# An attention and feed-forward kernel: the attention stage rewritten with raw pairwise transposes, K=64 scores and exponentials transposed on TensorE

## The chip, the cores and the metric

The kernel runs on one core of a Trainium2 chip. Its time is the device time of one execution in microseconds (us); lower is better. The kernel before was timed three times: 997.22, 1001.03 and 1001.95 us, with a median of 1001.03 us. Engine names are those of the profile: PE is TensorE's matrix multiply and PEld its weight load, DVE is VectorE, ACT is ScalarE, POOL is GpSimd, and SP is the queue from which the DMAs are issued. L12 is line 12 of the kernel that is spoken of.

## What is computed

There are 8 batches, 8 heads, 576 tokens and 64 columns per head. Each head's output mixes causal softmax attention with a read from a memory matrix, and the joined heads then pass through a feed-forward block.

```python
scores = scale * np.matmul(q, k.transpose(0, 1, 3, 2))      # scale = 1/8, causal mask, row maximum taken off
a = np.exp(scores)
a /= a.sum(-1, keepdims=True) + 1e-09
local = np.matmul(a, v)
q_p = phi(q)                                                # max(q, exp(q) - 1) + 1
mem_out = einsum(q_p, M_prev) / (einsum(q_p, z_prev) + 1e-06)
x = g * mem_out + (1 - g) * local                           # g = sigmoid(beta), per head
# feed-forward over 4608 tokens, 512 -> 1024 -> 512
h = x @ w_in
solu = h * softmax(h)
out = (layernorm(solu) * g_ln) @ w_out
```

The weights w_in and w_out arrive as float64 words, and the kernel decodes them itself.

## The kernel before

Attention is done for one pair of heads at a time: 32 pairs, four to a batch. Of the 576 tokens of a head, 512 form four blocks of 128 rows, and the last 64 rows of both heads form one shared "tail" block. Numbers that need more than one pass of precision are split into a high and a low part: `hi` and `lo` (L318 to L329) write the two parts of k, q and phi(q) side by side, so that a row has 64 high and 64 low columns and the contraction of a matmul is 128 deep.

One pair goes through these steps. `trans` (L437) transposes the split k, q and phi(q) on PE, 27 transposes of 128x128 (L447, L456), and ACT copies them out of PSUM (L433). `swap` makes a second copy of the transposed k with its halves exchanged, by a DMA (L469). `scores` (L523) multiplies q by k (L542) and by the exchanged k (L543); DVE adds the mask, negates, writes the scores to SBUF and finds the row maximum in one instruction (L546). `soft` (L482) takes the exponential and its row sum on ACT (L496), the scale from it on DVE (L500, L502), then the normalised high part in fp16 on POOL (L483) and the low part on DVE (L512), and transposes both by a DMA (L518). `values` (L602) multiplies by v, with v as the stationary operand (L608), and adds phi(q) times M_prev (L616, L635); the result has tokens in its columns, as the feed-forward's first matmul needs it. phi(q) has been divided by its norm beforehand (L348 to L366, on POOL and DVE). `merge` (L593) adds the high and low halves.

The feed-forward works on tiles of 128 tokens, 36 in all. For each, `g1` runs 24 matmuls with a moving operand of 512 columns into `h` (L683); a chain of single instructions follows, c1 to c10: maximum (DVE L698), exponential (ACT L704), product and sum (DVE L709), subtract the mean (POOL L718), squares (ACT L724), a power (POOL L728), the scaled high part (ACT L481) and low part (DVE L736), and a DMA transpose (L742). `g2` runs 24 more matmuls (L755).

Each engine executes its instructions in the order in which they were written. A virtual clock sets that order: `slot(p)` emits the scores of pair p, the values of pair p-1 and the preparation of pair p+1, and puts feed-forward steps in the gaps. Where each part falls is set by a table of fractions of a slot (P, L28 to L52) and of offsets (OFF, L53). PSUM has five banks that everything in attention shares in turn (`ps_s`), one bank for `g2`, and two banks for `h`. The weights are decoded by `weight_step` (L250) during the first slots, 24 chunks through a two-deep staging buffer.

Of the kernel before, what the change touches and what calls it, by code (L numbers as in the profile page):

```python
# [25 lines left out]
# Where the parts are emitted: fractions of a slot (of the slot before a pair's scores for its  # L26
# loads, preparation and transposes), and gaps of chains in us. They order the engines' work.
P = {  # L28
    "ld_k": -0.50, "ld_q": -0.40, "ld_v": -0.25, "ld_b": -0.22,
# [8 lines left out]
}  # L38
DEPS = (
    "ld_k k_hi k_lo tk0 tk1 tt swap", "ld_q q_hi q_lo phi3", "q_lo tt", "q_lo tq0 tq1", "ld_q phi1 phi2 phi3 phi4 phi5 p_hi p_lo tp0 tp1 tp2",  # L40
    "ld_v v1 v2 v3 v4 v5 v6", "v3 phi4", "ld_b m1", "s0 s1 s2 s3 st", "va vb vt", "ld_b phi3",
)
BUFS = {"pe": 5, "ksw": 2, "vst": 3, "mst": 2, "kT": 2, "qT": 2, "pT": 2, "ot": 2, "xf": 2, "lt": 2, "wt": 2}
OFF = {}
WT = ("lt",)
ENG = {"kst": "p", "qst": "p", "pst": "a", "lkst": "p", "lqst": "p", "lpst": "p", "relu": "a", "mx": "v", "v": "d", "h8": "p", "h6": "p", "h4": "p", "h2": "p", "h5": "p", "kT": "a", "qT": "a", "pT": "a", "xh": "a", "out": "a", "ln": "a"}
ENG0 = {}
EARLY = 5
WACT = 1
WPOOL = 1  # L50
P.update({'ld_k': -0.5, 'ld_q': -0.4, 'ld_v': -0.26061662954976644, 'ld_b': -0.1867630925796864, 'k_hi': 0.0, 'k_lo': 0.04, 'q_hi': 0.05, 'q_lo': 0.1, 'phi1': 0.12450449063930862, 'phi2': 0.19, 'phi3': 0.22023831229089622, 'phi4': 0.4, 'phi5': 0.49895318147926565, 'p_hi': 0.56, 'p_lo': 0.5448550353585894, 'v1': 0.01475376331245451, 'v2': 0.047523081121272154, 'v3': 0.12, 'v4': 0.5039851911500934, 'v5': 0.4742918073033215, 'v6': 0.54, 'm1': 0.48, 'tk0': 0.42010190124933844, 'tk1': 0.5017931553145808, 'tt': 0.5105694394820975, 'tq0': 0.56, 'tq1': 0.62, 'tp0': 0.8936934582661713, 'tp1': 0.9, 'tp2': 0.94, 'swap': 0.8808993830957448, 's0': 0.06, 's1': 0.20945219180060937, 's2': 0.4666999403328722, 's3': 0.61, 'sb': 0.04, 'st': 0.8, 'va': 0.07977765073539692, 'vb': 0.2, 'vt': 0.5125215606487175, 'ev': 0.4, 'e': 0.7129860651889, 'ex': 0.8, 'rr': 0.4, 'hi': 0.2752673338051288, 'lo': 1.41333215189741, 'tr': 1.24449487306772, 'mg': 0.2919189879262507, 'mg2': 0.6, 'xl': 0.8, 'c1': 0.2, 'c2': 1.3287303998695392, 'c3': 1.2, 'c4': 1.2, 'c5': 1.6217740235049547, 'c6': 1.1, 'c7': 0.4, 'c8': 0.6, 'c9': 1.1, 'c10': 0.6067076693930333, 'o1': 0.3, 'o2': 1.1498997242258686, 'low': 16.0, 'w0': 4.0, 'wmax': 3.483578790421383, 'wdec': 3.265097220718073, 'spl': 5.0})
# [12 lines left out]
def kernel(
    ctx: ExitStack,
# [843 lines left out]
```

## Time and profile before

| | |
|---|---|
| median of three runs | 1001.03 us |
| span of the profiled execution | 999.8 us |
| DVE busy | 888.1 us |
| PE busy | 809.1 us |
| ACT and POOL busy | 654.0 and 653.6 us |
| mean granted clock of PE | 0.899 |

The profile is of one execution; what lies around its span is not in it, and the span stands 1.2 us below the median. "Busy" is the time in which an engine has at least one instruction in work. The end of a matmul is modelled and includes the time to drain, so that neighbouring matmuls overlap in the rows: what a matmul costs PE is the distance between starts, or a run's length divided by its count. "Idle before" in a row is the engine's waiting ahead of these instructions, with what ended it.

### The profile page before, as it was taken

Reading aid. Unit: us, or ns where it says so; the run is one execution under the profiler, and the core shown is the slowest. Engines: PE = TensorE matmul, PEld = TensorE weight load, DVE = VectorE, ACT = ScalarE, POOL = GpSimd, SP = SyncE. Lnnn points to the kernel's source line nnn. Section 1 sums busy time; section 2 is a strip of 40 time slices with the busy share of each in tenths; the row PEclk is TensorE's granted clock in tenths of the full one; section 3 lists DMA queues with packets and bytes.
Section 4 is the critical chain, followed back from the end, with each engine's and each line's share of the span. In section 5 each row is a group of like instructions: output and inputs, shape, how many; then the busy total and the mean of one; then the engine's idle time right before and its main releaser. Section 6 shows DMA issues by size and latency. Waiting matters only on the chain. (4 is left out here: it accounts for less than half of the span.)

```text
span 999.8 us, 17169 instructions
## 1 busy us (share of the span) xinstructions
PE 809.1 (81%) x5313; PEld 591.3 (59%) x5313; DVE 888.1 (89%) x2181; ACT 654.0 (65%) x1507; POOL 653.6 (65%) x710
## 2 busy tenths in 40 slices
PE   0526686677679899898869998997879899899998
PEld 0424565555456576676656666756657666677663
DVE  6899999999998999999989999999999899998542
ACT  2636665745685677767656877677676777785543
POOL 3886667656786667776656767678767776774420
PEclk9956776877699899999988999999989999999999
DMA  6387998656688676787758778777867878747543
GB/s 153 110 181 179 179 201 176 130 114 145 122 162 174 134 143 129 161 170 148 143 104 164 151 150 167 157 149 152 161 124 166 171 151 163 141 98 144 102 85 85
DMA packets 423931, 145.85 MB, mean 146 GB/s; under 512 B 411040, under 2 KB 411040, under 8 KB 423840
## 3 DMA queue, kind: packets, MB, share of 16 engines
q1 hardware_dynamic: 423840, 144.76, 71.4%
q8 instruction: 42, 0.69, 0.3%
q14 instruction: 49, 0.40, 0.1%
HBM read 45.10 MB, written 9.44 MB: 55 GB/s over the span
## 5 line engine op out<-in xcount | busy, mean ns | idle before, releaser
L483 POOL TENSOR_SCALAR p<-pe,sm 128x512 f16<-128x512 f32 (+4 forms) x288 | 198.0, 698 | 122.3 <-DVE sm L502 46.1
L512 DVE SCALAR_TENSOR_TENSOR p<-pe,sm,p 128x512 f16<-128x512 f32 (+4 forms) x288 | 242.8, 858 | 19.7 <-POOL p L483 19.0
L496 ACT ACTIVATE pe<-pe,mn 128x512 f32<-128x512 f32 (+4 forms) x288 | 169.2, 588 | 134.4 <-DVE mn L546 98.6
L755 PE MATMUL g<-w,lt 128*128 128x512 f16 x816 | 203.9, 391 | 10.4 <-DMA lt<-ln 7.8
L608 PE MATMUL acc<-PT,vst 128*128 128x128 f16 (+1 forms) x1856 | 149.0, 229 | 26.0 <-DMA PT<-p 17.0
L608 PEld LDWEIGHTS <-vst 128*128 128x128 f16 x1856 | 112.2, 107 | 55.8 <-issue 45.2
L542 PE MATMUL sps<-kT,qT 128*128 128x512 f32 (+3 forms) x256 | 107.5, 424 | 40.7 <-DVE mn L546 20.2
L755 PEld LDWEIGHTS <-lt 128*128 128x128 f16 x864 | 78.8, 100 | 100.1 <-issue 15.2
L546 DVE CUSTOM_DVE_ANT_0 pe<-sps,maskbig 128x512 f32<-128x512 f32 (+3 forms) x256 | 120.5, 478 | 7.1 <-PE sps L543 6.0
L683 PE MATMUL h<-w1h,xh 128*128 128x512 f32 x272 | 115.1, 423 | 0.9 <-DVE e L714 0.6
L683 PE MATMUL h<-w1l,xh 128*128 128x512 f32 x272 | 110.8, 407 | 0.0
L683 PE MATMUL h<-w1h,xl 128*128 128x512 f32 x272 | 110.7, 407 | 0.0
L543 PE MATMUL sps<-ksw,qT 128*128 128x512 f32 (+3 forms) x256 | 92.7, 366 | 3.7 <-DMA ksw<-kT 3.7
L542 PEld LDWEIGHTS sps<-kT,qT 128*128 128x128 f32 x256 | 54.2, 212 | 57.8 <-DVE mn L546 24.8
L718 POOL TENSOR_SCALAR e<-e,s 128x1024 f32<-128x1024 f32 x36 | 41.3, 1147 | 64.7 <-DVE e L714 50.1
L447 PE MATMUL trp<-identr,pst 128*128 128x128 f32 x288 | 40.7, 274 | 46.2 <-POOL pst L327 24.9
L597 ACT ACTIVATE mtmp<-acc,sv 64x64 f32<-64x64 f32 (+1 forms) x128 | 63.5, 496 | 17.8 <-PE acc L608 11.6
L736 DVE SCALAR_TENSOR_TENSOR ln<-e,s,ln 128x1024 f16<-128x1024 f32 x36 | 51.7, 1437 | 18.1 <-ACT ln L481 18.0
L447 PEld LDWEIGHTS trp<-identr,pst 128*128 128x128 f32 x288 | 32.4, 150 | 54.8 <-POOL pst L327 26.3
L366 POOL TENSOR_TENSOR phi<-phi,nrm 128x576 f32<-128x576 f32 x32 | 45.4, 1420 | 28.6 <-DVE nrm L362 20.0
L683 PEld LDWEIGHTS h<-w1h,xh 128*128 128x128 f32 x272 | 52.7, 194 | 13.5 <-DVE s L709 2.0
L543 PEld LDWEIGHTS sps<-ksw,qT 128*128 128x128 f32 x256 | 55.7, 218 | 7.6 <-DMA ksw<-kT 3.7
(146 smaller groups left out, 2016.3 us busy)
## 6 DMA issues: line engine op xcount, KB each, us to landing
ksw<-kT SPq DMA_DIRECT2D x64, 288.0 KB, 4.2
qn<-in_q_dram SPq DMA_DIRECT2D x64, 128.0 KB, 2.8
vn<-in_v_dram SPq DMA_DIRECT2D x64, 128.0 KB, 2.7
kn<-in_k_dram SPq DMA_DIRECT2D x64, 128.0 KB, 3.2
wstage<-in_moe_w_out_dram SPq DMA_DIRECT2D x16, 512.0 KB, 4.5
out_dram<-ot SPq DMA_DIRECT2D x32, 256.0 KB, 2.4
wstage<-in_moe_w_in_dram SPq DMA_DIRECT2D x8, 512.0 KB, 4.6
PT<-p SPq DMA_TRANSPOSE x160, 3.7
```

The source lines that it names most:

```text
L447: nc.tensor.transpose(out=ps[:, j, :], in_=d[src][:, blk, :], identity=identr)
L483: (nc.vector if e == "v" else nc.gpsimd).tensor_scalar(out=out, in0=in_, scalar1=scale, scalar2=0.0, op0=ALU.mult, op1=ALU.add)
L496: nc.scalar.activation(out=pe[:, :n], in_=pe[:, :n], func=ACTF.Exp, scale=-1.0, bias=mn, accum_out=sm[:, i:i + 1])
L512: nc.vector.scalar_tensor_tensor(out=p16[:, w * i:w * i + w, 1, :], in0=parts[i][1][:, :n].rearrange("p (w c) -> p w c", c=128), scalar=sm ...
L542: nc.tensor.matmul(out=ps[:, :n], lhsT=lhs, rhs=d["kT"][:, a, :], start=True, stop=False)
L543: nc.tensor.matmul(out=ps[:, :n], lhsT=lhs, rhs=d["ksw"][:, a, :], start=False, stop=True)
L546: nc.vector.tensor_tensor_reduce(out=pe[:, :n], in0=ps[:, :n], in1=maskbig[:, SM + 128 - n:], scale=-0.125, scalar=BIG, op0=ALU.add, op1=A ...
L597: nc.scalar.activation(out=tmp[a, :n], in_=acc[c, cols], func=ACTF.Copy, scale=sc[c])
L608: nc.tensor.matmul(out=acc[:, cols], lhsT=vs[:, blk, :], rhs=pt[:, pi + c, rows], start=start and c == 0, stop=stop and c == 1)
L683: nc.tensor.matmul(out=o, lhsT=t[a][:, kk, :], rhs=w[:, kk, c], start=(kk == 0 and n == 0), stop=(kk == KM - 1 and n == 2))
L736: nc.vector.scalar_tensor_tensor(out=ln[:, :, 1, :], in0=e.rearrange("p (k c) -> p k c", c=128), scalar=s4[:, 3:4], in1=ln[:, :, 0, :], op ...
L755: nc.tensor.matmul(out=t["o"], lhsT=t["lt"][:, 2 * kk + a, :], rhs=w2[:, kk, w, :], start=(kk == 0 and n == 0), stop=(kk == KF - 1 and n = ...
```

## The change

The whole of the attention code is replaced, with the order of the work.

k and q are transposed as they were loaded, for both heads of a pair in one 128x128 fp32 transpose (L272 of the changed kernel). The split in high and low parts happens when ACT and DVE take the result out of PSUM. The scores are three matmuls with a contraction of 64 for each head and block: q high by k high, q low by k high, q high by k low. The mask is added by a matmul with an identity. DVE then only finds the maximum (L328), and ACT takes the exponential straight from PSUM (L330), without a row sum. The fp32 exponentials are transposed on PE (`trans`, L363), and ACT and DVE split them into fp16 parts as they take them out (L366, L367). The values have the exponentials as the stationary operand and v with a column of ones as the moving one, so that the row sum comes out of the same matmul; the memory read is an unsplit fp32 matmul with an added column for its norm (L399). DVE normalises both at the output (L404 to L417) and POOL adds them. Tokens now lie in rows, so the feed-forward transposes its input first (`ff_split`, L425). The swap DMA, the 160 DMA transposes of the exponentials, and most of POOL's work are gone. The feed-forward has one `h` and one `g` buffer for all tiles.

```diff
-P = {
-    "ld_k": -0.50, "ld_q": -0.40, "ld_v": -0.25, "ld_b": -0.22,
...
+SLOT = 20000
+LAG = 6
+BUFS = {
...
+    "ph": 2, "pht": 2, "E": 5, "pt": 7, "x1": 2, "x2": 2, "X": 8, "Xt": 2,
+    "xh": 2, "xl": 2, "xth": 1, "xtl": 1, "e": 2, "ln": 2, "lt": 2, "ot": 1,
+}
...
+    def prep_qk(p):
...
+            for j in range(NM):
+                nc.tensor.transpose(out=ps[:, 128 * j:128 * j + 128], in_=d[nm + "n"][:, j].rearrange("p h d -> p (h d)"),
+                                    identity=identf)
...
+            copy(h, ps, sc)
+            rest(l, ps, h.bitcast(F32), sc)
...
+    def unit(p, blocks):
...
+            for x, (a, c) in enumerate((("qh", "kh"), ("ql", "kh"), ("qh", "kl"))):
+                for hh in range(2):
+                    r = slice(64 * hh, 64 * hh + 64)
+                    mm(ps[hh][:, o:o + n], d[a][r, 128 * i:128 * i + 128], d[c][r, 0:n],
+                       start=(x == 0 and i == blocks[0]), stop=False)
+            for hh in range(2):
+                mm(ps[hh][:, o + 128 * i:o + n], identb, maskd, start=False, stop=True)
...
+                nc.vector.tensor_reduce(out=nm[:, x, hh:hh + 1], in_=ps[hh][:, c], axis=AX.X, op=ALU.max, negate=True)
+            for hh in range(2):
+                nc.scalar.activation(out=e[hh][:, c], in_=ps[hh][:, c], func=ACTF.Exp, bias=nm[:, x, hh:hh + 1])
...
+    def trans(p, keys):
...
+            nc.tensor.transpose(out=ps[:, 128 * x:128 * x + 128], in_=d.pop(("src",) + key), identity=identf)
+        t = buf([128, 2, 4, 128], F16, "pt")
...
+        copy(tv[:, 0, :128 * n], ps[:, :128 * n], ES)
+        rest(tv[:, 1, :128 * n], ps[:, :128 * n], tv[:, 0, :128 * n], ES)
...
+            mm(acc[:, o:o + 65], t[:, 0], vs[:, j, hh, 0:65], start=first and j == 0, stop=False)
+            mm(acc[:, o:o + 64], t[:, 0], vs[:, j, hh, 66:130], start=False, stop=False)
+            mm(acc[:, o:o + 65], t[:, 1], vs[:, j, hh, 0:65], start=False, stop=(j == js[-1]))
...
+            mm(acm[:, 130 * x:130 * x + 130], lhs, d["b"]["mz"][:, hp, :], start=(x == 0), stop=True)
...
+    for n, (kind, i) in enumerate(seqw):
+        at(n * SLOT // 4)
+        weight_load(n, i)
...
+        at(t0)
+        unit(p, [3])
+        at(t0 + 2000)
+        trans(p, [(3, 0, j) for j in range(4)])
+        trans(p, [(3, 1, j) for j in range(4)])
+        at(t0 + 4000)
+        unit(p, [2])
...
```

The new code only sets priorities (`at`), from which a scheduler makes each engine's order. Three places show what became of it. Names: `wt`, `w1h` are the weights under decoding, `kT`, `trp`, `kh`, `trk` the transposed keys in SBUF and PSUM, `sps` the scores, `E` their exponentials, `etr` and `pt` the transposed exponentials in PSUM and SBUF, `h` and `g` the feed-forward's two results.

On ACT, at the start of the program, before:

```order
L375 ACTIVATE vst,mx<-vn 128x9x64
L184 ACTIVATE ig<-bt 128x8
L407 ACTIVATE vst<-vn,sv 128x9x64
L229 ACTIVATE wt<-wt 128x512 x2
L375 ACTIVATE vst,mx<-vn 128x9x64
L273 ACTIVATE w1h<-wt 128x512
L433 ACTIVATE kT<-trp 128x512 x2
```

and in the changed kernel:

```order
L170 ACTIVATE wt<-wt 128x512 x2
L108 ACTIVATE w1h<-wt 128x512 x2
L170 ACTIVATE wt<-wt 128x512 x2
L108 ACTIVATE w1h<-wt 128x512 x2
L170 ACTIVATE wt<-wt 128x512 x2
L108 ACTIVATE w1h<-wt 128x512 x2
L170 ACTIVATE wt<-wt 128x512 x2
L108 ACTIVATE w1h<-wt 128x512 x2
L170 ACTIVATE wm<-wm 128x8
L170 ACTIVATE wt<-wt 128x512
L108 ACTIVATE kh<-trk 128x512
```

The first key copy came after one chunk of weights; now it comes after all eight chunks of w_in, the maximum over the eight chunks of w_out (`wm`) and the first decoding step of w_out.

On PE, in the middle of the program, before:

```order
L683 MATMUL h<-w1h,xh 128x512
L447 MATMUL trp<-identr,kst 128x128 x4
L456 MATMUL trp<-identr,kst 128x128
L456 MATMUL trp<-identr,qst 128x128
L683 MATMUL h<-w1h,xl 128x512
L683 MATMUL h<-w1l,xh 128x512
L683 MATMUL h<-w1h,xh 128x512
L542 MATMUL sps<-kT,qT 128x256
L543 MATMUL sps<-ksw,qT 128x256
L683 MATMUL h<-w1h,xl 128x512
```

and in the changed kernel, in the last pair of a batch:

```order
L105 MATMUL sps<-kl,qh 128x512 x2
L105 LDWEIGHTS identb
L105 MATMUL sps<-maskd,identb 128x128
L105 LDWEIGHTS identb
L105 MATMUL sps<-maskd,identb 128x128
L363 MATMUL etr<-identf,E 128x128 x8
L105 MATMUL sps<-kh,qh 128x384 x2
L105 MATMUL sps<-kh,ql 128x384 x2
L105 MATMUL sps<-kl,qh 128x384 x2
```

From the second batch on, feed-forward matmuls stood between the steps of attention in every pair. Now the last two pairs of each batch (and all four of the first batch) have none: the transposes of a block's exponentials stand right behind that block's scores, and the next block's scores behind them. The first two pairs of batches 1 to 7 hold the previous batch's four or five tiles, in runs of up to 24 matmuls; at the end of each batch PE has the transposes of `ff_split` for the whole batch, then the first tile's `g1`; the last batch's tiles follow its attention.

On DVE, before:

```order
L546 ISA pe,mn_4894<-sps,maskbig 128x512
L546 ISA mn_4894 128x1
L388 TENSOR_SCALAR sv<-sv 128x1
L546 ISA pe,mn_4923<-sps,maskbig 128x512
L546 ISA mn_4923 128x1
L359 TENSOR_SCALAR nrm<-nrm,sv 128x9
L512 SCALAR_TENSOR_TENSOR p_4846<-pe,sm,p_4846 128x5x128
```

and in the changed kernel, in a pair without feed-forward:

```order
L328 TENSOR_REDUCE nm_4434<-sps 128x1 x2
L112 SCALAR_TENSOR_TENSOR vst_97<-vn_95,sv,vst_97 128x10x64
L221 SCALAR_TENSOR_TENSOR ph<-trq,ph 128x512
L112 SCALAR_TENSOR_TENSOR pt<-etr,pt 128x512 x2
L328 TENSOR_REDUCE nm_4467<-sps 128x1 x2
L112 SCALAR_TENSOR_TENSOR pt<-etr,pt 128x384 x2
L328 TENSOR_REDUCE nm_4506<-sps 128x1 x4
```

The maxima of a block (`nm`) now stand behind the taking-out of the block before it (`pt`), where the scores of one block used to stand beside the softmax of another.

More of the change, by code (lines that the diff above doesn't have):

```diff
@@ L44 @@
[L44 to L51, printed above, removed]
@@ L128, in buf @@
+    et = [const.tile([128, SM + 128], F32, name=f"et{i}") for i in range(2)]
     def buf(shape, dtype, tag, name=None):
         return sb.tile(shape, dtype, tag=tag, name=name or tag, bufs=BUFS.get(tag, 1))
[L133 to L146 removed]
@@ L148, in drain, with bank, at @@
[L148 to L160 removed]
+    def bank(name):
+        return ps_s.tile([128, 512], F32, tag="s", name=name)
+    def at(t):
+        tc.cur_priority = int(t) + 200000
@@ new lines, in prep_v @@
+    def prep_v(p):
+        d = st[p]
+        hp = p % HP
+        o = d["vst"] = vst[p % 2]
+        x = d["vn"].rearrange("p t h d -> p (t h) d")
+        oh = o.rearrange("p t h d -> p (t h) d")
+        m = tiny.tile([128, 1], F32R, tag="mx", name="mx", bufs=4)
+        with nc.allow_low_precision("only a scale comes from it"):
+            nc.scalar.activation(out=oh[:, :, 0:D].bitcast(BF16), in_=x, func=ACTF.Abs, accum_out=m)
+        ps = bank("mps")
+        nc.tensor.matmul(out=ps[:, :128], lhsT=m.to_broadcast([128, 128]), rhs=identr, start=True, stop=True)
+        s = tiny.tile([128, 4], F32, tag="sv", name="sv", bufs=4)
+        nc.vector.tensor_reduce(out=s[:, 0:1], in_=ps[:, :128], axis=AX.X, op=ALU.max)
+        nc.vector.tensor_scalar(
+            out=s[:, 0:1], in0=s[:, 0:1], scalar1=2.0 ** -14, scalar2=1e-30, op0=ALU.mult, op1=ALU.max)
+        nc.vector.reciprocal(out=s[:, 1:2], in_=s[:, 0:1])
+        nc.vector.tensor_scalar(
+            out=s[:, 2:4], in0=io[:, 2 * hp:2 * hp + 2], scalar1=s[:, 1:2], scalar2=None, op0=ALU.mult)
+        d["iop"] = s[:, 2:4]
+        copy(oh[:, :, 0:D], x, s[:, 1:2])
+        rest(oh[:, :, 66:130], x, oh[:, :, 0:D], s[:, 1:2])
@@ new lines, in ff_split, with ff_g1 @@
+                rest(t["xl"][r, :, o:o + 64], pv[r, :, 64 * hh:64 * hh + 64], t["xh"][r, :, o:o + 64].bitcast(F32))
+    def ff_g1(t):
+        h = t["h"] = ps_h.tile([128, DFF], F32, tag="h", name="h")
+        for nh in range(2):
+            c = slice(nh * 512, nh * 512 + 512)
+            for kk in range(KM):
+                for n, (a, w) in enumerate((("xh", w1h), ("xl", w1h), ("xh", w1l))):
+                    nc.tensor.matmul(out=h[:, c], lhsT=t[a][:, kk, :], rhs=w[:, kk, c],
+                                     start=(kk == 0 and n == 0), stop=(kk == KM - 1 and n == 2))
@@ new lines, in ff_g2 @@
+    def ff_g2(t, rows):
+        o = ps_g.tile([128, DM], F32, tag="g", name="g")
+        for kk in range(KF):
+            for n, (a, w) in enumerate(((0, 0), (1, 0), (0, 1))):
+                nc.tensor.matmul(out=o, lhsT=t["lt"][:, 2 * kk + a, :], rhs=w2[:, kk, w, :],
+                                 start=(kk == 0 and n == 0), stop=(kk == KF - 1 and n == 2))
+        ot = buf([128, DM], F32, "ot")
+        copy(ot, o, wsc[:, 2:3])
+        for r0, pr in rows:
+            nc.sync.dma_start(out=out[r0:r0 + pr.stop - pr.start, :], in_=ot[pr, :])
```

899 lines of the change are left out of this document (290 added, 609 removed), and 9 rows, old and new, of tables (BUFS, P).

## The prediction

> **What bounds the kernel now.** I read the page's busy times first, then the stretches (windows), then the groups by form for prices, and last the chain that ended last.
>
> ```profile
> PE 809.1 (81%) x5313; PEld 591.3 (59%) x5313; DVE 888.1 (89%) x2181; ACT 654.0 (65%) x1507; POOL 653.6 (65%) x710
> ...
> L483 POOL TENSOR_SCALAR p<-pe,sm 128x512 f16<-128x512 f32 (+4 forms) x288 | 198.0, 698 | 122.3 <-DVE sm L502 46.1
> L512 DVE SCALAR_TENSOR_TENSOR p<-pe,sm,p 128x512 f16<-128x512 f32 (+4 forms) x288 | 242.8, 858 | 19.7 <-POOL p L483 19.0
> ```
>
> DVE is busy for 888.1 of 999.8 us, so the old kernel is close to DVE's own time. The two groups below the first row are the normalising and splitting that the change removes from POOL and DVE.
>
> ```profile
> 60.00:120.00 60.00, 35.57 (x232) 28.60 (x232) 58.35 (x143) 35.85 (x89) 43.42 (x45) 0.65 0.85 179
> ...
> 250.00:500.00 250.00, 215.40 (x1445) 155.85 (x1444) 231.44 (x567) 176.38 (x411) 177.32 (x190) 0.91 0.74 149
> ```
>
> The columns are the stretch's length, the busy time of PE, PEld, DVE, ACT and POOL, then PE's clock. In the middle DVE is busy for 93% and PE for 86%: feed-forward beside attention keeps both full. Early, with attention alone, PE is busy for 59% at a clock of 0.65. So the questions are what the new work costs each engine, and whether the new order still lets one engine work while another does.
>
> **What the change removes and adds, by engine.**
>
> ```profile
> L546 DVE CUSTOM_DVE_ANT_0 pe<-sps,maskbig 128x512 f32<-128x512 f32 x64 | 43.3, 677 | 0.9 <-PE sps L543 0.8
> L387 DVE TENSOR_REDUCE sv<-mps 128x1 f32<-128x128 f32 x32 | 9.0, 280 | 0.7 <-PE mps L383 0.7
> L433 ACT ACTIVATE kT<-trp 128x512 fp32r<-128x512 f32 x64 | 37.5, 588 | 15.4 <-PE trp L447 12.0 <-DMA kn<-in_k_dram 2.9
> L433 ACT ACTIVATE pT<-trp 128x128 fp32r<-128x128 f32 x32 | 8.8, 274 | 2.6 <-PE trp L447 2.6
> ```
>
> *DVE.* From PSUM, 512 columns take 677 ns and 128 take 280 ns: 0.148 us and 1.034 ns per column. A pair now has 26 large instructions with 9,920 columns (maxima 3,072, exponentials' low parts 3,200, k, q and phi 1,536, v 640, normalising 1,280, the rest 192): 26 x 0.148 + 9,920 x 0.001034 = 14.1 us, and some 1.9 us of tiny ones: 16 us a pair, 512 us for 32. With 36 feed-forward tiles at 4.8 us (rows below, and 0.7 us for the input's low part), some 55 us for the weights (16 chunks at 2.65 us, worked out below, and the maxima) and an estimated 20 us of work per batch, the sum is 760 us against 888. POOL falls to a fraction. *ACT*, by the same reading of its two rows (0.169 us and 0.82 ns per column), needs 12 us a pair, 610 us in all. Neither is the bound.
>
> ```profile
> 937.67 5.34 PE h L683 x23
> ...
> 948.13 5.20 PE g L755 x24
> 558.09 0.63 PEld L447 LDWEIGHTS trp<-identr,pst 128*128 128x128 f32 x5
> 558.67 0.19 PEld L683 LDWEIGHTS h<-w1h,xh 128*128 128x128 f32 x1
> 518.33 0.41 PE L608 MATMUL acc<-PT,vst 128*128 128x64 f16 x8
> 518.57 0.28 PE L635 MATMUL acc<-pT,mst 128*128 128x64 f32 x1
> 518.69 0.41 PE L608 MATMUL acc<-PT,vst 128*128 128x64 f16 x8
> ```
>
> *PE.* At full clock a 512-column fp32r matmul takes 0.232 us (5.34/23), an fp16 one 0.217. Five transposes' loads take 0.63 us, of which the last takes a load's own 0.19, so each follows by 0.11. Nine matmuls of 64 columns start within 0.36 us: 0.04 each. A pair's 24 score matmuls, six of each width, cost 6 x (0.232 + 0.174 + 0.116 + 0.11) = 3.8 us if the two heads' K=64 matmuls go one after the other; the masks 0.6; the tail 1.0; 33 transposes 3.6; 75 value matmuls 3.0; five fp32 memory matmuls and the scale's 2.4. That is 14.4 us, 461 for all pairs. A tile costs 5.6 + 5.2 + 0.4 for its input's transposes = 11.2 us, 403 for all. So PE's own work is about 870 us.
>
> Two of these prices no row shows. No fp32 (not fp32r) operand occurs in the trace: a transpose lies between 0.11 us, the fp32r price, and 0.44, four trips of that price, as the four products of high and low halves in L542 and L543 make up one full product. I take 0.11, since a transpose only moves values and the fp32r row moves equally wide ones; the memory matmul multiplies, and I take the upper end, 0.44. No K=64 matmul occurs either: two heads may share the array at once, which takes off at most half of 3.8 us a pair, 61 us in all, or not at all. I take a third of it, 18 us. The Trainium skill ("TensorE: Matmul & The Clock Gate", Part 3, Packing small matmuls) has matmuls in different row groups run concurrently; by it, the whole 61 us would go. No run so far shows it.
>
> **Where the time goes: waits.** The shares say 870 us, but the order does not let PE have it.
>
> *Start.*
>
> ```profile
> 0.71 1.45 SPq L298 DMA_DIRECT2D tqn<-in_q_dram  x2
> 8.85 1.05 SPq L215 DMA_DIRECT2D wstage<-in_moe_w_in_dram  x2
> 16.42 0.43 DVE L257 TENSOR_SCALAR wt<-wstage 128x512 int32<-128x512 int32 x1 [1.43 <-DMA wstage<-in_moe_w_in_dram]
> 19.52 0.68 DVE L260 SCALAR_TENSOR_TENSOR wt<-wstage,wt 128x512 f32<-128x512 uint32 x1
> 34.37 0.76 PE L542 MATMUL sps<-kT,qT 128*128 128x512 f32 x1
> wstage<-in_moe_w_out_dram SPq DMA_DIRECT2D x16, 512.0 KB, 4.5
> ```
>
> The old kernel's first scores start at 34.37 us. The new ACT order has the first key copy behind eight decoded chunks, eight loads for the maximum and one more decoding. Some 24 DMA issues at 0.62 us precede the first weights (15 us), which land 7.6 us later (8.85 to 16.42): 22 us. Two chunks are in flight; a round of two is 5.3 us on DVE (three steps of 0.43 and two of 0.68 each), with POOL behind it and a 4.5 us load before the next: 8.5 us, four rounds, 34. The maxima go two per load time, about 5.5 us, four rounds, 22. First scores then stand at about 80 us. The loads of k and q have long landed; nothing hides this.
>
> *A pair without feed-forward (18 of 32).* PE's order is scores, their transposes, the next scores, so each block's chain is open. From the pair's transposes (in us): key and query copies on ACT and low parts on DVE, last scores 4.3; behind the previous pair's normalising on DVE, two maxima, 6.1; exponential and eight transposes, 7.2; on DVE v, phi and two low parts stand ahead of the next maxima, which end at 10.2; exponentials, transposes, 11.1; 16 score matmuls, 12.6; four maxima 14.2; tail scores 15.0; their maximum 16.0; exponential 17.0; transposes, values and memory 20.7. DVE works 16 of these 20.7 us. About 9 us of the path are PE's, and at clocks as in 60 to 120 us they stretch: 23.5 us. Batch 0: 80, a first pair of 45 (half of the weights' decoding still goes through DVE), three of 23.5: 195.
>
> *Pairs with feed-forward.* A tile's chain:
>
> ```profile
> L698 DVE TENSOR_REDUCE nm<-h 128x1 f32<-128x1024 f32 x34 | 41.3, 1214 | 6.1 <-PE h L683 5.9
> L704 ACT ACTIVATE e<-h,nm 128x1024 f32<-128x1024 f32 x34 | 37.8, 1113 | 26.9 <-DVE nm L698 26.6
> L709 DVE CUSTOM_DVE_ANT_0 e<-h,e 128x1024 f32<-128x1024 f32 x34 | 41.3, 1216 | 3.0 <-ACT e L704 2.8
> L718 POOL TENSOR_SCALAR e<-e,s 128x1024 f32<-128x1024 f32 x36 | 41.3, 1147 | 64.7 <-DVE e L714 50.1
> L724 ACT ACTIVATE ln<-e 128x1025 bf16<-128x1025 f32 x36 | 38.1, 1057 | 17.1 <-POOL e L718 16.8
> L728 POOL TENSOR_TENSOR s<-s,neghalf 128x1 f32<-128x1 f32 x36 | 24.5, 681 | 14.2 <-ACT ln L724 13.8
> L481 ACT ACTIVATE ln<-e,s 128x1024 f16<-128x1024 f32 x36 | 41.2, 1144 | 9.1 <-POOL s L728 9.1
> L736 DVE SCALAR_TENSOR_TENSOR ln<-e,s,ln 128x1024 f16<-128x1024 f32 x36 | 51.7, 1437 | 18.1 <-ACT ln L481 18.0
> lt<-ln SPq DMA_TRANSPOSE x36, 4.4
> ```
>
> These sum to 13.4 us, about 15 with hops and small steps; the first three hold `h`, which the next tile's g1 needs, for 4.5 us with hops. In the first two pairs of a batch PE has 2 x 14.4 + 3.5 tiles of 11.2 = 68 us of work. Its order puts the first tile's g2 12 us of work behind its g1, so 3 us are waited; the second costs 1.5; where the fills run out in the second pair, an open attention chain costs 5. Sum 78. The batch's end adds 13: the last values must be normalised before `ff_split` (2.8 + 2.5 us), twenty transposes go through five banks (about 3), and g1 takes 5.6. A batch is 78 + 47 + 13 = 138; seven are 966, and 24 more for the fifth tile that three of them carry.
>
> *End.* Five tiles of the last batch follow alone. With one `h`, g1 waits 4.5 us for the tile before, and g2 15 us for its own: the last g2 ends 71 us after the first g1, with 8.5 + 5.6 before and 3 after it: 88 us.
>
> **The sum.** 195 + 990 + 88 = 1273 us, less 18 for the K=64 pairs: **1255 us**, made against the span of 999.8; the 1.2 us to the median are inside its roundness. That is 25% slower. DVE stops being the bound, and waiting in order takes its place.
>
> **The rivals.**
>
> (1) *Faster: PE packed full.* If the two heads' matmuls share the array and the transposes of a block never wait, a batch falls to PE's work, 4 x 12.5 + 4.5 x 11.2 = 100.4 us, and the time to 185 + 703 + 88 = 976. It is faster only from below 101.7 us a batch. For it: 86% PE busy in the middle of the old trace. Against it: in that stretch 86% came with attention of two pairs interleaved, which the new order doesn't have. Chance 0.04.
>
> (2) *DVE-paced attention.* If DVE finds its next work at once, a pair without feed-forward takes about 17 us and the laden ones lose no more than now: 195 + 7 x 125 + 24 + 70 = 1164. It lies in the range. Chance 0.15.
>
> (3) *fp32 transposes at four times the price.* 33 transposes at 0.33 us more, 25 of them on the open path, are 8.3 us a pair, 264 us, and 160 input transposes some 30 more: about 1540. Against it: equal width in the fp32r row. The Trainium skill ("FP8 and Floating Point Precision", TensorE Precision Notes) has true fp32 take four passes, while its "TensorE: Matmul & The Clock Gate" (Terms) names a transpose mode that is four times faster for fp32. No run so far shows either. Chance 0.12.
>
> **How the numbers follow.** The forecast has 0.69. Its own range is 1150 to 1400: below by the full 61 us and waits a tenth shorter, above by hops of 0.2 us at each of some 20 links a pair. With rival 2 the range is 1120 to 1420; what it leaves out is rivals 1 and 3 and a few per cent. Faster by over 0.5% (about what a measurement of this kernel can tell from no change) is rival 1, 0.04; within it 0.01; slower 0.95.
>
> **What would show it.** In the new profile: first scores near 80 us; PE and DVE both under 75% busy; the tenths of PE low for about two pairs in four; waits of PE's transposes on ACT's exponentials, and of `g` on the DMA `lt`, at the top of the list; a spacing near 0.11 us between fp32 transposes; 20 to 25 us between the scores of pairs without feed-forward. I am wrong if PE is over 90% busy, if the first scores come before 50 us, if transposes follow by 0.4 us, or if a pair without feed-forward takes under 17 us.

## The result, and the profile after

The changed kernel takes 1246.41 us (median of four runs, 1243.91 to 1252.07) where the kernel before takes 1000.65 (997.22 to 1001.95): 1.246 times as long, 95% interval 1.2416 to 1.2505. The forecast was 1255 us. The profiled execution has a span of 1242.1 us. From the page, and from the stretches (columns as in the prediction: length, busy time of PE, PEld, DVE, ACT and POOL, PE's clock):

```profile
PE 990.6 (80%) x7457; PEld 705.0 (57%) x7457; DVE 692.2 (56%) x1533; ACT 590.4 (48%) x1108; POOL 171.6 (14%) x275
```

```profile
60.00:120.00 60.00, 29.82 (x192) 21.56 (x192) 47.55 (x107) 24.73 (x48) 12.50 (x14) 0.83 0.46 132
250.00:500.00 250.00, 213.59 (x1654) 153.11 (x1653) 142.05 (x320) 127.93 (x244) 30.36 (x54) 0.86 0.23 51
276.84:300.03 23.19, 18.49 (x175) 14.48 (x172) 14.10 (x36) 12.18 (x24) 2.15 (x5) 0.71 0.15 33
555.46:576.17 20.71, 15.54 (x175) 12.46 (x172) 13.89 (x36) 12.17 (x24) 2.16 (x5) 0.92 0.17 38
```

DVE is relieved as the change says: 692.2 us in place of 888.1. Nothing of that reaches the time. Between 250 and 500 us DVE works 142 us where it worked 231, and PE is busy for as long as before, 214 us against 215, at a clock of 0.86 in place of 0.91. The last two rows are two pairs without feed-forward, the third of batch 1 and of batch 3, with the same work: 23.2 us at a clock of 0.71, 20.7 at 0.92. PE's waits, with what ended them (us in all, times, longest):

```profile
PE etr L363 <- ACT E L330: 94.3, 65, 4.0
PE wps L179 <- DVE wmx L177: 74.4, 1, 74.4
...
PE g L484 <- DMA lt<-ln: 25.9, 13, 8.4
```

PE waits for the exponentials `E` ahead of their transposes, once for 74.4 us at the start, and for the transposed feed-forward tiles. On PE's timeline, the start and the pair of 23.2 us:

```profile
74.36 0.48 PE L179 MATMUL wps<-identr,wmx 128*128 128x128 f32 x1 [74.36 <-DVE wmx L177]
...
75.06 0.47 PE L272 MATMUL trk<-identf,kn 128*128 128x128 f32 x1
...
80.91 0.80 PE L105 MATMUL sps<-kh,qh 64*128 64x512 f32 x2 [0.75 <-ACT qh L108]
...
280.13 1.23 PE L363 MATMUL etr<-identf,E 128*128 128x128 f32 x8 [1.71 <-ACT E L330]
281.29 0.47 PE L105 MATMUL sps<-kh,qh 64*128 64x384 f32 x2
...
283.89 1.54 PE L363 MATMUL etr<-identf,E 128*128 128x128 f32 x6 [1.16 <-ACT E L330]
...
288.77 0.69 PE L363 MATMUL etr<-identf,E 128*128 128x128 f32 x2 [0.92 <-ACT E L330]
```

The first instruction in PE's queue is `wps`, the matmul of the weights' scale (L179). It needs all eight maxima of `w_out`, so even the first transposes of k and q stand behind the weights until 75 us. In the pair, PE waits 1.71, 1.16 and 0.92 us for exponentials, each time with the next block's scores queued behind the transposes that wait. The clock's record in the trace holds two values only, full and half. In this pair it is half from 281.6 to 295.2 us, that is, from shortly behind the first of these waits.

### The profile page after: what moved, and what is told of

Its sections match the earlier page's. It is cut to its first block, busy times and chain, and to the rows that moved or that the text cites. A ratio compares the mean times of both kernels' runs of the same rounds, so it can differ in the third digit from the quotient of the medians.

```text
span 1242.1 us, 19040 instructions
## 1 busy us (share of the span) xinstructions
PE 990.6 (80%) x7457; PEld 705.0 (57%) x7457; DVE 692.2 (56%) x1533; ACT 590.4 (48%) x1108; POOL 171.6 (14%) x275
## 5 line engine op out<-in xcount | busy, mean ns | idle before, releaser
L108 ACT ACTIVATE pt<-etr 128x512 f16<-128x512 f32 (+1 forms) x224 | 119.4, 550 | 196.1 <-PE etr L363 194.1
L112 DVE SCALAR_TENSOR_TENSOR pt<-etr,pt 128x512 f16<-128x512 f32 (+1 forms) x224 | 136.9, 629 | 133.1 <-ACT pt L108 131.0
L363 PE MATMUL etr<-identf,E 128*128 128x128 f32 x640 | 130.2, 335 | 94.3 <-ACT E L330 94.3
L330 ACT ACTIVATE E<-sps,nm 128x512 f32<-128x512 f32 (+3 forms) x256 | 124.6, 525 | 89.9 <-DVE nm L328 88.9
L363 PEld LDWEIGHTS etr<-identf,E 128*128 128x128 f32 x640 | 88.4, 169 | 121.0 <-ACT E L330 113.4
L105 PE MATMUL acc<-vst,pt 128*128 128x65 f16 (+1 forms) x2880 | 126.4, 203 | 18.3 <-ACT pt L108 15.6
L328 DVE TENSOR_REDUCE nm<-sps 128x1 f32<-128x512 f32 (+3 forms) x256 | 115.7, 485 | 44.9 <-PE sps L105 37.0
L105 PEld LDWEIGHTS <-pt 128*128 128x128 f16 x2880 | 116.3, 104 | 36.8 <-ACT pt L108 24.1
L105 PE MATMUL sps<-kh,qh 64*128 64x512 f32 (+3 forms) x256 | 69.1, 463 | 7.9 <-DVE sv L294 5.6
L461 DVE TENSOR_REDUCE s<-h 128x1 f32<-128x1024 f32 x36 | 43.9, 1220 | 35.2 <-PE h L453 34.7
L179 PE MATMUL wps<-identr,wmx 128*128 128x128 f32 x1 | 0.5, 476 | 74.4 <-DVE wmx L177 74.4
L105 PE MATMUL acm<-mz,ph 128*128 128x130 f32 x256 | 58.4, 364 | 0.6 <-ACT E L330 0.6
```

Of the source, the lines that this page charges most:

```text
L105: nc.tensor.matmul(out=out, lhsT=lhsT, rhs=rhs, start=start, stop=stop, skip_group_check=True)
L108: nc.scalar.activation(out=out, in_=in_, func=ACTF.Copy, scale=scale)
L112: nc.vector.scalar_tensor_tensor(out=out, in0=in_, scalar=1.0 if scale is None else scale, in1=hi, op0=ALU.mult, op1=ALU.subtract)
L328: nc.vector.tensor_reduce(out=nm[:, x, hh:hh + 1], in_=ps[hh][:, c], axis=AX.X, op=ALU.max, negate=True)
L330: nc.scalar.activation(out=e[hh][:, c], in_=ps[hh][:, c], func=ACTF.Exp, bias=nm[:, x, hh:hh + 1])
L363: nc.tensor.transpose(out=ps[:, 128 * x:128 * x + 128], in_=d.pop(("src",) + key), identity=identf)
```

## The experiments

My theory after the result was the prediction's: the order makes PE wait, at the start and in every open chain. The main rival was that PE's own work at the granted clock is the bound (990.6 us busy, 80%), so that order does not matter. Differences below are against 1246.41; the ratios are to the kernel before.

### The start

`weights` is called behind score block x of pair p; `issue_after(newest(e))` puts what follows behind the newest instruction of that engine.

```diff
-    for n, (kind, i) in enumerate(seqw):
...
+    def weights(p, x):
...
+            for e in (ET.PE, ET.DVE, ET.Activation):
+                s.enter_context(tc.issue_after(newest(e)))
...
+            for n in (8 * p + 2 * x, 8 * p + 2 * x + 1):
```

> Edit: the 24 weight steps are no longer ahead of the first pair; two of them stand behind each score block of pairs 0 to 2, on PE, DVE and ACT. My theory (the start is a queue wait, nothing hides it): first scores near 18 us in place of 80.9, but pairs 0 to 2 now carry the weights' 55 us of DVE work beside 14 us of their own each, so they take about 33 us each in place of 37.8, 26.1 and 21.7; net -63 + 14 = -49 us, about 1197. Rival (the weights' DVE work is a cost of its own, wherever it stands): pairs 0 to 2 become DVE's and take 14 + 18 + chain = 40 us or more each, and less than 20 us is gained, 1225 or more.

This run takes 1206.18 us, a ratio of 1.204 (1.2019 to 1.2061) and 40.2 us less. The first scores start at 12.71 us in place of 80.91, and the first three pairs take 36.9, 38.1 and 38.7 us. The third of them:

```profile
87.70:126.40 38.70, 22.59 (x178) 18.19 (x174) 36.99 (x88) 19.90 (x39) 10.31 (x11) 0.56 0.35 106
```

DVE works 37.0 of its 38.7 us. The stall was a queue's, as the theory says, but part of the rival holds: of the 68 us that the first scores came earlier, 28 are paid again in pairs that DVE now fills.

### Feed-forward spread over all four pairs

`ff_tile` holds what the loop in `ff_batch` did for one tile; `ff_due` is called behind each block of a pair and issues the tile that is due there.

```diff
-            at(t1)
-            ff_g1(tt)
...
+            n = 5 * HP * x // len(todo)
+            held[HP * b + HP + n // 5, n % 5] = (b, x, len(todo), i, tt, rows)
...
+    def ff_due(p, n):
+        f = held.pop((p, n), None)
+        if f:
+            with tc.issue_after(newest(ET.PE)):
+                ff_tile(*f)
```

> Edit: the feed-forward tiles of a batch may no longer all be issued in the first two pairs of the next batch; tile x is held back on PE to its quarter (or fifth) of the four pairs. The work is the same. My theory (pairs without feed-forward wait in open chains, 5 us each, and their clock falls): with a tile beside each pair the waits fill, a batch falls from 138 to about 118 us, seven times 20 is 140, time about 1105. Rival (PE's own work at the granted clock is the bound, PE being busy for 80% of the span): the same work in another order takes the same time, 1230 to 1250.

This run takes 1224.71 us, a ratio of 1.2249 (1.2204 to 1.2294) and 21.7 us less, near the rival's figure and far from the theory's 1105. The waits say why:

```profile
PE etr L363 <- ACT E L330: 85.3, 62, 4.0
```

PE now waits 85.3 us in 62 waits, where it waited 94.3 us in 65. A tile's matmuls fill only the wait in which they happen to stand. In the pair that starts at 358.4 us they stand between the scores of block 3 and their transposes, which wait for nothing; the transposes of block 2 and of block 1 still follow their scores directly and wait 1.66 and 0.97 us. Of the 60 waits over 0.2 us, 44 are of that second kind. Work beside a chain does not fill the chain's waits; it has to stand in them.

### The next block's scores first

```diff
         at(t0 + 2000)
+        unit(p, [2])
+        at(t0 + 4000)
         trans(p, [(3, 0, j) for j in range(4)])
         trans(p, [(3, 1, j) for j in range(4)])
-        at(t0 + 4000)
-        unit(p, [2])
         at(t0 + 6000)
+        unit(p, [1, 0])
+        at(t0 + 8000)
         trans(p, [(2, 0, j) for j in range(3)])
         trans(p, [(2, 1, j) for j in range(3)])
-        at(t0 + 8000)
-        unit(p, [1, 0])
```

> Edit: the scores of block 2 are issued ahead of the transposes of block 3, and those of blocks 1 and 0 ahead of the transposes of block 2. My theory (open chains): each of the two waits of 1.6 us for the exponentials in a pair without feed-forward is covered by 1.6 us of scores, so 2 to 3 us go from 17 of the 32 pairs, and about as much again of the start of each laden one; -40 to -70 us, about 1190. Rival (PE's work is the bound): the waits only move to the next place, within 15 us of 1246.

This run takes 1123.40 us, a ratio of 1.1224 (1.117 to 1.1278) and 123 us less, twice what I expected. The wait, and a pair without feed-forward:

```profile
PE etr L363 <- ACT E L330: 8.4, 16, 0.9
```

```profile
254.70:272.37 17.67, 15.56 (x174) 12.37 (x174) 13.38 (x33) 11.44 (x23) 2.74 (x5) 1.00 0.22 54
```

The waits for exponentials fall from 94.3 to 8.4 us, 86 us. Most of the other 37 come from the same instructions running faster: PE's busy time falls by 33, from 990.6 to 957.1 us, at a mean clock of 0.955 in place of 0.870. The rival falls: no work was removed.

### How much the two heads share

```diff
-            for x, (a, c) in enumerate((("qh", "kh"), ("ql", "kh"), ("qh", "kl"))):
-                for hh in range(2):
+            for hh in range(2):
+                for x, (a, c) in enumerate((("qh", "kh"), ("ql", "kh"), ("qh", "kl"))):
```

> Edit: the three K=64 score matmuls of one head stand behind each other, then those of the other head, where the heads took turns. Same instructions. Theory from the changed kernel's trace (a pair of 384-column K=64 matmuls follows the pair before after 0.17 us, as long as one of them): matmuls of the two heads share the array in full, and without turns each pair of heads loses about 1.5 us of PE work at full clock, on the open path: 32 x 1.5 / 0.87 = +55 us, about 1300. Rival, as the prediction had it (a third of the sharing is had): +18 us, about 1264. Second rival (scores hide behind other engines): no change.

This run takes 1246.95 us, a ratio of 1.2453 (1.2427 to 1.2479), which is no change. The edit did not undo what it was meant to undo, as PE's timeline of that run shows:

```profile
494.52 0.45 PE L105 MATMUL sps<-kh,qh 64*128 64x384 f32 x2
494.80 0.34 PE L105 MATMUL sps<-kh,ql 64*128 64x384 f32 x2
494.97 0.34 PE L105 MATMUL sps<-kl,qh 64*128 64x384 f32 x2
```

In PE's program the three matmuls of one head now stand ahead of those of the other. In the trace the two heads still run side by side (x2 in each row), and a pair of 384 columns follows the last after 0.17 us. The next run takes the shared rows away instead:

```diff
-                    r = slice(64 * hh, 64 * hh + 64)
+                    r = slice(0, 64)
```

> Edit: the score matmuls of both heads read rows 0 to 63, so that the second head's scores are left out (the first head's are computed twice) and the two can no longer share the array; number, shapes and order stay. In the run with one head after the other the trace still showed the two heads' matmuls starting 4 to 10 ns apart and a pair of 384 columns taking 0.17 us, so that run did not undo the sharing; this one does. Theory (the sharing is full and lies on the open path): 1.6 us more of PE work at full clock in each of 32 pairs, 51 us, and the lower clock makes it 55 to 65: about 1305. Rival, as the prediction had it (a third is had, 18 us): about 1265. Second rival (scores hide behind other engines): no change.

This run takes 1311.93 us, a ratio of 1.311 (1.3036 to 1.3184) and 65.5 us more. In that run two such matmuls take twice as long:

```profile
523.47 0.61 PE L105 MATMUL sps<-kh,qh 64*128 64x384 f32 x2
523.93 0.51 PE L105 MATMUL sps<-kh,ql 64*128 64x384 f32 x2
524.27 0.51 PE L105 MATMUL sps<-kl,qh 64*128 64x384 f32 x2
```

From row to row it is 0.34 us against 0.17. The sharing is full.

### What the waits do to the clock

```diff
+    def fill(p, n):
+        if p % HP > 1:
+            t = ps_g.tile([128, DM], F32, tag="g", name="fill")
+            for _ in range(n):
+                mm(t, identr, st[p]["kh"], start=True, stop=True)
...
         unit(p, [3])
+        fill(p, 4)
...
         unit(p, [2])
+        fill(p, 4)
...
         unit(p, [1, 0])
+        fill(p, 2)
```

> Edit: in the third and fourth pair of each batch, 4, 4 and 2 matmuls of 512 columns that nobody reads stand where PE waits for the exponentials of block 3, block 2 and blocks 1 and 0. Work is only added, 0.93, 0.93 and 0.46 us at full clock in waits of 1.7, 1.6 and 1.0 us. Theory (the waits cost twice, since the granted clock falls where PE is idle: 0.66 to 0.92 in such pairs, 1.00 in the run with the next scores first): the pairs without feed-forward go from 20.7 to 24.9 us to about 20.5 at a clock near 1.00, 16 pairs of 2 to 3 us are 30 to 50 us, about 1205. Rival (the clock falls for another reason, the K=64 or the fp32 instructions): the clock stays, and at such a clock the added work outlasts the waits: those pairs 0 to 1.5 us longer, 1246 to 1270.

This run takes 1257.42 us, a ratio of 1.2565 (1.2522 to 1.2608) and 11 us more. It decided nothing, since the fills had not stayed in their places. In the third pair of batch 3:

```profile
555.61 1.97 PE L105 MATMUL fill<-kh,identr 128*128 128x512 f32 x6
558.04 1.25 PE L369 MATMUL etr<-identf,E 128*128 128x128 f32 x8 [0.46 <-ACT E L330]
...
561.78 1.37 PE L369 MATMUL etr<-identf,E 128*128 128x128 f32 x6 [1.56 <-ACT E L330]
```

Six stand ahead of the first transposes, none ahead of the second, where 1.56 us are still waited. The pair of this run that the next expectation calls one with all fills in place, the third of batch 1 (282.2 to 302.5 us), has six ahead of the first transposes and none ahead of the second as well, where it waits 1.55 us; its clock stayed at 1.00 all the same, where the pair above has 0.73. The next run ties each fill behind its scores and the transposes behind the fill:

```diff
+            with tc.issue_after(newest(ET.PE)):
+                for _ in range(n):
+                    mm(d["fill"], identr, d["kh"], start=True, stop=True)
+            x.enter_context(tc.issue_after(newest(ET.PE)))
...
+        with fill(p, 4):
             at(t0 + 2000)
             trans(p, [(3, 0, j) for j in range(4)])
```

> Edit: as in the run before, 4, 4 and 2 unread matmuls of 512 columns in the waits for the exponentials of the third and fourth pair of each batch, but tied to their places: that run had put six ahead of the first transposes, none ahead of the second and four ahead of the next pair's scores. There the one pair with all fills in place took 20.2 us at a clock of 1.00, the same pair without fills 23.2 at 0.71. Theory (the waits cost twice, since the granted clock falls where PE is idle): third pairs go from 20.7 to 24.9 us (clock 0.66 to 0.92) to 20 to 21 (near 1.00); over 16 pairs 25 to 45 us less, about 1210. Rival (the clock falls for another reason): clock as before, those pairs 0 to 1.5 us longer, 1246 to 1270.

This run takes 1178.92 us, a ratio of 1.1792 (1.1764 to 1.1819) and 67.5 us less than the changed kernel, with 160 matmuls more. I had expected 25 to 45 us. The pair that took 23.19 us, and the start of it on PE's timeline:

```profile
270.00:289.63 19.63, 16.62 (x187) 12.39 (x184) 14.18 (x37) 12.05 (x24) 2.15 (x5) 1.00 0.19 44
```

```profile
271.39 1.18 PE L105 MATMUL fill<-kh,identr 128*128 128x512 f32 x4
273.29 1.23 PE L375 MATMUL etr<-identf,E 128*128 128x128 f32 x8 [0.72 <-ACT E L330]
```

The wait ahead of the transposes is 0.72 us in place of 1.71, the clock stays at 1.00, and the pair is 3.6 us shorter although it holds ten matmuls more. Eight third pairs go from a mean of 23.1 to 19.7 us and seven fourth pairs from 34.6 to 30.5: 56 of the 67 us. That the lower clock follows from PE's waits is shown by this run together with the one with the next scores first, whose pair of 17.67 us keeps a clock of 1.00 with the same K=64 and fp32 instructions and nothing added; the rival (another reason) falls. How long or how many the waits must be is not shown.

### The edits together

The next run holds the edits of the first and the third run, the one after it those of the first three.

> Edit: both at once, the weights behind the blocks of pairs 0 to 2 and the next block's scores ahead of the transposes. If the two causes (start, open chains) are independent their gains add: 1123 - 40 = 1083. If they share something (the first three pairs are DVE's with the weights, so that order no longer helps there): the 7 + 1 + 5 us that the order gained in pairs 0 to 2 are lost, about 1097.

The run with two of the edits takes 1090.18 us, a ratio of 1.091 (1.0853 to 1.0966), between the two figures. Pairs 0 to 2 take 29.6, 30.3 and 43.9 us; in the third, PE stands 17.3 us before the scale's matmul:

```profile
PE wps L179 <- DVE wmx L177: 17.3, 1, 17.3
```

> Edit: the weights behind the blocks, the next block's scores first, and the feed-forward tiles spread over the four pairs. Spreading alone gave 22 us, as PE's waits for the exponentials stayed (85 us against 94) and the clock rose to 0.893. Theory (the fill helps only where a chain is open, and the order of the scores has closed most of them): next to nothing beside the run with two of the edits, within 20 us of it. Rival (laden pairs are still too long because the tiles are bunched): 40 us or more faster than that run, below 1050.

With all three edits it takes 1145.14 us, a ratio of 1.1433 (1.139 to 1.1475), 55 us slower than without the spreading. Both sides of my expectation were wrong. Between 500 and 750 us, first in the run with two edits, then in this one:

```profile
500.00:750.00 250.00, 236.74 (x1923) 170.27 (x1922) 157.42 (x360) 139.97 (x274) 34.20 (x60) 0.97 0.27 59
```

```profile
500.00:750.00 250.00, 229.35 (x1707) 160.42 (x1708) 142.07 (x320) 126.30 (x246) 31.80 (x53) 0.88 0.24 53
```

PE waits 7 us more in 250, and loses the clock again, 0.88 for 0.97. Which of the waits brings that about (the tiles' own transposes now take score banks in the middle of pairs) was not tried and stays open.

The last three runs leave the tiles bunched, with the scores first. The weights' steps are spread over pairs 0 to 3; m counts the score blocks, four to a pair:

```diff
+            if m == 8:
+                at(2 * SLOT)
+                weight_scale()
+            for n in (2 * m, 2 * m + 1) if m < 8 else (m + 8,):
```

> Edit: scores first as before, and the weights' steps spread evenly: one chunk of w_in and one maximum behind each score block of pairs 0 and 1, the scale behind the first block of pair 2, one chunk of w_out behind each block of pairs 2 and 3, so that no pair carries more than 13 us of them. Theory (the first pairs are DVE's: 14 us of their own and 13 of weights): pairs 0 to 3 take about 27, 27, 28 and 32 us where the run with two chunks behind each block took 29.6, 30.3, 43.9 and 37.0; the next batch starts near 127 in place of 153, time about 1064. Rival (the wait for the scale of the weights at the third pair, 17 us, is a load's and not DVE's): only a few us, above 1080.

This run takes 1083.24 us, a ratio of 1.0834 (1.0801 to 1.0867). Pairs 0 to 3 take 28.4, 32.1, 37.6 and 38.4 us, not 27 to 32, and the time is where the rival had put it, above 1080. The third pair:

```profile
73.00:110.50 37.50, 22.84 (x173) 17.41 (x173) 35.10 (x81) 19.44 (x37) 13.60 (x14) 0.60 0.44 138
```

The rival's reason is not the one: DVE works 35.1 of the 37.5 us and hardly waits for a load. DVE is the pace, as the theory has it, but carries more than the 27 us that I had counted: a chunk of `w_out` takes it 3.7 us (six steps of 0.41 to 0.83), and the steps of six chunks lie in this pair, two of them left over from the pair before. To this a second `h` is added at the end, in the score banks (`scores` is their pool):

```diff
+        if b == B - 1:
+            for bb, i, tt, rows in todo[:NM]:
+                ff_split(bb, i, tt)
+            scores.close()
+            hs.append(pool("ps_h2", 1, PS))
...
+        hs.append(hs.pop(0))
+        h = t["h"] = hs[0].tile([128, DFF], F32, tag="h", name="h")
```

> Edit: the same, and in the last batch the score banks are given up for a second h, so that the first matmuls of a tile no longer wait for the tile before. Theory (the tail is a queue of chains: PE waits there 3.9 us for h and 2.5, 3.0 and 8.4 us for transposed tiles, 18 of 88 us): with four tiles' first matmuls ahead the only wait left is part of the last one, 4 to 9 us, so the tail is 10 to 14 us shorter than in the run beside it, about 1052. Rival (the tail is the last tile's own chain, 15 us from its h to its g): 3 us or less.

This run takes 1070.26 us, a ratio of 1.0729 (1.069 to 1.0768), 13.0 us less than the run beside it, as forecast. Over the whole run, PE's waits for transposed tiles fall from 19.1 us to 5.7 (in all, times, longest):

```profile
PE g L488 <- DMA lt<-ln: 5.7, 6, 1.6
```

In the tail they fall from 14.1 us to the 1.6 us ahead of the last tile's `g`, less than the 4 to 9 us expected.

And the scale of the weights is moved back by two blocks:

```diff
-            if m == 8:
+            if m == 10:
...
-            for n in (2 * m, 2 * m + 1) if m < 8 else (m + 8,):
+            for n in ((m + 6,) if 9 < m < 14 else (2 * m - 8, 2 * m - 7) if m > 13 else () if m > 7 else (2 * m, 2 * m + 1)):
```

> Edit: as the run before (scores first, weights spread, two h at the end), but the scale of the weights, with its matmul on PE, stands behind the third score block of the third pair, and the chunks of w_out move to the last blocks of pairs 2 and 3. Theory (one matmul that waits for DVE holds up the queue behind it: PE stood 10.1 us before the scale's matmul in the third pair, and the clock was 0.57 to 0.61 there): the 10 us go, of which DVE, busy for 37.5 of 40 us there, takes half back; about 1062. Rival (pairs 0 to 3 are DVE's through and through, whatever PE waits for): within 4 us of 1070.

This run takes 1067.54 us, a ratio of 1.0639 (1.0606 to 1.0672), the rival's side: 2.7 us less, which is inside the spread of the two kernels' runs. PE waits 6.2 us for the scale in place of 10.1, and the next batch starts at 149.8 us in place of 147.3. DVE is busy for 113 us of pairs 0 to 3 in both runs, so most of their time is DVE's, if not all of it as the rival has it. No version tried comes below the kernel before; this one is 6.4% above it. Its batches 1 to 6 take 123.0 us each; the first takes 149.8, and the last with the tail takes 180.6. What would shorten those two further was not tried.

## Why the prediction was right, and where it was not

| Step | Predicted | Profile after |
|---|---|---|
| First scores | 80 us | 80.9 |
| First pair | 45 | 37.8 |
| Pair without feed-forward | 23.5 | 23.4 (mean of nine, 20.7 to 26.1) |
| First two pairs of a batch | 78, and 3.4 for fifth tiles | 80.0 (mean of seven) |
| End of a batch, beyond its fourth pair | 13 | 11.2 (34.6 - 23.4) |
| Tail, from the last batch's input transposes | 88 | 88.2 (1153.9 to 1242.1) |
| PE's work at full clock | 870 | 862 (990.6 x 0.870) |
| DVE, ACT | 760, 610 | 692, 590 |

**The mechanism held.** DVE stopped being the bound and waiting in order took its place. The run with the next scores first removes nothing but waits and takes 123 us off. The profile shows the signs that were named: first scores near 80 us, PE's transposes waiting for ACT's exponentials and `g` for the DMA `lt` at the top, and 20.7 to 26.1 us for a pair without feed-forward, where 20 to 25 was named.

**The start** came out at the right time with one cause too few. The prediction gave ACT's order, with the key copy behind the decoded chunks. PE's own first instruction, `wps`, waits for the same weights and holds the transposes too; I had not read PE's first row. By the order of the queues either alone would have kept the pair waiting; the two were not separated on the chip. The first pair was 7 us shorter than forecast.

**The sharing of K=64 matmuls was mis-sized.** The step was "I take a third of it, 18 us". All of it is had: 65.5 us in time when it is taken away, a little more than the 61 us of work, with the clock at 0.841 in place of 0.870. The Trainium skill's rule ("TensorE: Matmul & The Clock Gate", Part 3, Packing small matmuls: matmuls in different row groups run concurrently) agrees with the trace, 0.17 us for a pair of 384 columns against 0.34 in the same rows.

**The clock was mis-sized the other way**, and the two errors partly covered each other. The walk through a pair gave 20.7 us at full clock, with the two heads' scores one after the other. With full sharing that is 19.1; the run with placed fills, where the clock is 1.00, takes 19.6. What lifts it to 23.4 is 3.8 us of lower clock, where the prediction added 2.8. Its own row would have given more: 9 us of PE's path at the clock of 0.65 that it names are 4.8 us longer (9 / 0.65 - 9). That the sum, 1255, is only 9 us from the median is in part luck. With the full 61 us of sharing, the steps' 1273 us would have come to 1212, 30 us below the profiled 1242. The clock makes up 18 of these 30 in the pairs without feed-forward (18 times 1.0 us); where the other 12 lie was not taken apart.

**Two signs were wrong by the letter.** PE is busy for 80%, not under 75%: busy time is counted at the granted clock, and 862 us at full clock would be 69%. For the same reason the tenths of PE are not low in two pairs of four; they read mostly 7 to 9, with PE slow more than idle. A busy share without the clock beside it takes a slow PE for a full one. The 862 is an estimate, as not all of PE's time follows the clock: for the same instructions the same product is 914 us in the run with the next scores first (957.1 x 0.955).

**The prices.** Transposes in fp32 follow each other by 0.12 us at full clock, and the fp32 memory matmul costs about twice as much:

```profile
486.96 1.04 PE L363 MATMUL etr<-identf,E 128*128 128x128 f32 x8
487.93 0.44 PE L105 MATMUL sps<-kh,qh 64*128 64x384 f32 x2
...
549.00 0.91 PE L105 MATMUL acm<-mz,ph 128*128 128x130 f32 x6
549.75 0.44 PE L105 MATMUL acc<-vst,pt 128*128 128x65 f16 x9
```

Eight transposes take 0.97 us (487.93 - 486.96), 0.12 each and near the fp32r price of 0.11: rival 3 falls. Three memory matmuls, recorded as six instructions, take 0.75 us: 0.25 each, under the 0.44 that I took. By the prediction's 0.232 for 512 columns, 130 columns of fp32r would be 0.059; but a matmul that loads weights of its own, as a transpose does, follows by 0.11. Two recorded instructions at that distance make up most of the 0.25, so this row can't tell longer multiplying from two loads. The Trainium skill ("TensorE: Matmul & The Clock Gate", Terms) names a transpose mode that is four times faster for fp32, and the 0.12 us agrees with it. The four passes for true fp32 of the Trainium skill ("FP8 and Floating Point Precision", TensorE Precision Notes) are neither shown nor refuted by the 0.25 us.

The value matmuls are 90 a pair, not 75 (2880 in all); at 0.03 us each their sum is still near 3 us. DVE's PSUM prices held (`pt<-etr` of 512 columns: 688 ns). The 68 us too many lie mostly in the pairs: DVE works 14.1 and 13.9 us in the two that are shown, where 16 were reckoned, and 32 times 2 is 64. The exponentials' low parts have not left DVE, as the prediction's first reading suggests; they take 136.9 us there now, where L512 took 242.8.

**The rivals.** DVE-paced attention (17 us a pair) shows only once the order is mended: 17.67 us then, PE busy for 15.6 of them and DVE for 13.4, so it is still not DVE's. PE packed full needed less than 101.7 us a batch (103 with the 185 us that the prediction itself gives the first batch there); with the scores first a batch takes 123 (181.96 to 922.22 us for six), so even the mended order is not on that side.

## What to carry to other kernels

A wait of PE can cost twice: its own length, and the clock of what comes after it (here 86 us and 33 us). Count a chain's waits at PE first, and put work between a producer's scores and the consumer's transposes in PE's own order; work that merely belongs to the same stretch does not fill them. When a change relieves the busiest engine, look for the first row of each queue and the open chains before counting the relief as time.

## What the runs showed of the hardware

PE's granted clock fell in stretches where no single wait was longer than 1.7 us: a pair with waits of 1.71, 1.16 and 0.92 us had 0.71, the same pair with 0.72 us ahead of the same transposes had 1.00, and 160 added matmuls made the kernel 67.5 us faster. The length of the waits does not fix the loss: the pair of 20.7 us has waits of 1.70, 1.57 and 0.97 us and was at half clock for 3.4 us only, where the pair of 23.2 us was for 13.7. The Trainium skill ("TensorE: Matmul & The Clock Gate", Why this matters for your kernels) warns of idle gaps over about 3 us; here shorter ones sufficed, and the measurement decides.

Matmuls that use rows 0 to 63 and rows 64 to 127 overlapped in full even when PE's program held three of one kind ahead of three of the other: 0.17 us from pair to pair and 1246.95 us in all, as with turns. The Trainium skill ("TensorE: Matmul & The Clock Gate", Part 3, The mechanism) has matmuls start in strict program order. In this trace the second head's first matmul starts 10 ns after the first head's first and 270 ns ahead of the first head's second, so between matmuls in different row groups that order does not hold, nor does the rule that each engine executes its instructions as they were written.
